# Four small moves in the backward pass of a two-layer linear-attention and gated-GLU kernel: filler units, small products, and a bank for the last quarter

## The chip, the cores and the metric

The kernel runs on one core of one Trainium2 chip. The metric is the device time of one execution in microseconds. Three runs of the kernel before gave 1201.79, 1202.06 and 1202.13 us, so the median is 1202.06 us.

## The reference

The reference computes a forward pass over a sequence of 2048 rows of width 512 and all gradients of it. The forward pass is four residual layers, A, B, A, B, that share one set of weights for A and one for B. Cut to what matters:

```python
def A(x, wqkv, wo):                     # 32 heads of 16, no softmax
    q, k, v = split_heads(x @ wqkv)
    pq, pk = phi(q), phi(k)             # phi: t+1 if t>0 else exp(t), plus 1e-6
    kv = einsum("sd,se->de", pk, v)     # per head
    den = pq @ pk.sum(s) + 1e-6
    return merge_heads((pq @ kv) / den) @ wo

def B(x, wg, wu, wd):                   # hidden width F = 1376
    return (sigmoid(x @ wg) * (x @ wu)) @ wd

x = x + A(ln(x)); x = x + B(ln(x)); x = x + A(ln(x)); x = x + B(ln(x))
return x, vjp(grad_out) w.r.t. x, wqkv, wo, wg, wu, wd
```

All inputs and outputs are bf16. Since layers 0 and 2 share their weights, and layers 1 and 3 theirs, each weight gradient is a sum over two layers.

## The kernel before, in words

The 2048 rows are cut into 16 row tiles of 128 (`st`). The residual stream and, later, its gradient stay in SBUF in float32; what the backward pass needs of each layer is stored to HBM in the forward pass.

The backward pass goes through layers 3, 2, 1, 0. `b_bwd_p1` (layers 3 and 1) and `a_bwd_p1` (layers 2 and 0) carry the gradient of x through a layer, one row tile after another. The weight gradients need all 16 row tiles of a layer at once. They are computed by one object, `W` of class `P2`, which holds a list of jobs and cuts each into **units**: sixteen matmuls of 256 or 96 columns for `wu`, `wg` and `wqkv`, eight of 512 columns for `wd`. `W.run(n)` emits the next n units at that place of the program. So units serve as filler: one is put wherever the chain of a layer would make TensorE wait. Two units in a row (a half job) share one PSUM tile of the pool `u`, which has two. After the second of them the tile is evacuated: by ScalarE (line 1386) where the result is a partial sum to be stored in HBM, by VectorE (line 1384) where it is the final one and the partial sum of the other layer is added. The result tile `dw_stg` has two buffers and is stored when its job is done, and the operand `p_set` of a job (1 MB for 256 columns) has three buffers and is loaded two jobs ahead.

All engines but SyncE run in the order in which the program text emits instructions (`tc.manual_schedule`), so the order written out by hand is the order on the chip. All DMAs are issued by SyncE (SP), in an order that the framework chooses at build time; an SP instruction that waits holds up those behind it.

The places that the change touches:

- `a_bwd_p1`, second half. `chain_mm(i, "N")` and `chain_mm(i, "M")` make two 512x512 products (line 1598, line 1602) in four tiles each, taken in turn from the pools `g` and `t`; the tiles are copied to SBUF by ScalarE and VectorE in turn (lines 362 and 364). Then the loop over row tiles begins with transposes into a tile of pool `t` (line 1649), a copy by ScalarE that seeds a tile of pool `g` (line 1633), and matmuls that add to that seed (line 1653). In its first pass one unit follows (line 1673).
- `b_bwd_p1`, layer 1. A row tile begins with three products `dhh` of 512, 512 and 352 columns (line 1059, "slices" 0, 1, 2) into the two tiles of pool `g`, each read twice by VectorE (line 1067). In the first row tile two units follow after the third slice and two more after the first transposes.
- The end of the program. After layer 0 the remaining units run without a chain beside them, 58 of them after the last loads: 42 of `wu`/`wg` (the last eight of 96 columns) and 16 of `wqkv`. Among them stand eight small products `sg` (`a_small_grads`: lines 1719 and 1728, into pool `t`, evacuated by ScalarE to a two-buffer tile `fin_o` at lines 1721 and 1731, then stored at 1722 and 1732).
- The very last job is `split`: its third and fourth quarter (16 matmuls each) are evacuated and stored on their own, but both lie in one PSUM tile (lines 1404 to 1413).

Of the kernel before, what the change touches and what calls it, by code (L numbers as in the profile page):

```python
# [10 lines left out]
F32 = mybir.dt.float32  # L11
# [11 lines left out]
P = 128  # L23
NST = S // P
NDC = D // P
# [37 lines left out]
def ps_tile(k, which, shape, dt, name):  # L63
    return k.ps[which].tile(shape, dt, name=name, tag="ln_tp" if which == "ln" else f"{which}_ps")
# [3 lines left out]
def kernel(  # L68
# [22 lines left out]
    k = K()  # L91
# [147 lines left out]
    if True:  # L239
        def load_b_weights():  # L240
            k.wdT = wb.tile([P, NDC, F], BF16, name="wdT", tag="w_c")
            nc.sync.dma_start(out=k.wdT[:], in_=k.wT["wdT"].rearrange("(c p) f -> p c f", p=P))
            k.wuT = wb.tile([P, NFC, D], BF16, name="wuT", tag="w_a")
            k.wgT = wb.tile([P, NFC, D], BF16, name="wgT", tag="w_b")
            for t_sb, t_d in ((k.wuT, k.wT["wuT"]), (k.wgT, k.wT["wgT"])):
                nc.sync.dma_start(out=t_sb[:], in_=t_d.rearrange("(c p) j -> p c j", p=P))

        def load_a_weights(l):
            woT_GT = wb.tile([P, 2, NDC, D], BF16, name="woT_GT", tag="w_b")
            k.woT, k.GT = woT_GT[:, 0, :, :], woT_GT[:, 1, :, :]  # L250
            nc.sync.dma_start(out=k.woT, in_=k.wT["woT"].rearrange("(c p) j -> p c j", p=P))
            k.wqkvT = wb.tile([P, 3 * NDC, D], BF16, name="wqkvT", tag="w_a")
            nc.sync.dma_start(out=k.wqkvT[:], in_=k.wT["wqkvT"].rearrange("(c p) j -> p c j", p=P))
            MT_X = wb.tile([P, 2, NDC, D], BF16, name="MT_X", tag="w_c")
            k.MT, k.X_ld = MT_X[:, 0, :, :], MT_X[:, 1, :, :]
            nc.sync.dma_start(out=k.MT, in_=k.sv[l]["MT"].rearrange("(c p) j -> p c j", p=P))
            nc.sync.dma_start(out=k.X_ld, in_=k.sv[l]["X"].rearrange("(c p) j -> p c j", p=P))
        k.load_b_weights, k.load_a_weights = load_b_weights, load_a_weights

        bconst = bctx.enter_context(tc.tile_pool(name="bconst", bufs=1, reuse_waits="tile"))  # L260
        k.ident32 = bconst.tile([P, P], F32, name="ident32")
        nc.gpsimd.memset(k.ident32[:], 0.0)
        nc.gpsimd.affine_select(out=k.ident32[:], in_=k.ident32[:], compare_op=ALU.not_equal, fill=1.0,
                                base=0, pattern=[[-1, P]], channel_multiplier=1)
        k.e0 = bconst.tile([P, P], BF16, name="e0")
        nc.gpsimd.memset(k.e0[:], 0.0)
        nc.gpsimd.memset(k.e0[0:1, :], 1.0)
        R = P2Res(k,
                  big=bctx.enter_context(tc.tile_pool(name="p2pool", bufs=1, reuse_waits="tile")),
                  sets=bctx.enter_context(tc.tile_pool(name="p2sets", bufs=3, reuse_waits="tile")),  # L270
                  stage=bctx.enter_context(tc.tile_pool(name="p2stage", bufs=2, reuse_waits="tile")),
                  set_w=2 * P)
        def mk_out1_cb(o1stg):
            o1cur = {}

            def out1_cb(st):
                if st % 2 == 0:
                    o1cur["t"] = o1stg.tile([P, 2, D], BF16, name="out1_t")
                nc.gpsimd.tensor_scalar(o1cur["t"][:, st % 2, :], k.xs[st][:], 1.0, 0.0, ALU.mult, ALU.add)
                if st % 2 == 1:  # L280
                    nc.sync.dma_start(out=dram_batch(out1, st // 2, 2), in_=o1cur["t"][:])
            return out1_cb

        W = P2(k, R)

        def mid3(st):
            if 4 <= st < 8:
                W.load(3, "g", part=st - 4)
            elif st == 8:
                W.add(b_jobs(k, 3), 3, False)  # L290
            elif 9 <= st < 13:
                W.load(3, "h", part=st - 9)

        def mid1(st):
            if 6 <= st < 10:
                W.load(2, "h", part=st - 6)
            elif st == 11:
                W.add(a_jobs(k, 2), 2, False)

        b_bwd_p1(k, 3, W, mid3)  # L300
        prectx.close()
        a_bwd_p1(k, R, 2, W)
        W.run(W.left() - HOLD)
        b_bwd_p1(k, 1, W, mid1)
        W.add(b_jobs(k, 1), 1, True)
        a_bwd_p1(k, R, 0, W, mk_out_cb=mk_out1_cb)
        tail = bctx.enter_context(tc.tile_pool(name="t_big", bufs=1, reuse_waits="tile"))
        W.add(a_jobs(k, 0), 0, True, split=True)
        with tc.manual_schedule(engines=EM):
            W.run(W.left() - 58)  # L310
            W.load(0, "h", tail)
            W.run(10)
            sg = a_small_grads(k, tail, R.stage)
            next(sg)
            W.run(20)
            for _ in sg:
                W.run(2)
            W.run(W.left())


# [52 lines left out]
def dram_batch(ap2d, b, nb=NB):  # L373
    return ap2d[batch_rows(b, nb), :].rearrange("(n p) d -> p n d", p=P)
# [714 lines left out]
def b_bwd_p1(k, l, W, mid):  # L1089
    nc, tc = k.nc, k.tc  # L1090
    sv = k.sv[l]
    first = k.g_from_input == l
    if not first:
        k.load_b_weights()
    with ExitStack() as ctx:
# [93 lines left out]
        def last_transposes(T):  # L1189
            transposes(T, 2)  # L1190
            store(T)
# [10 lines left out]
        for st in range(NST):  # L1202
            load(st + 1)
            ssd, h_st = LD.pop(st)
            T = dict(st=st, h=h_st, ssd=ssd, dd=halved(st, "dd", wide))
            T["ddT"] = wide.tile([P, 2, NFC, P], BF16, name="ddT")
            for fs in range(2):
                if not (first and st == 0):
                    dd_ops(k, T["dd"], T["ssd"], fs, dhh_mm(k, gTs[st], fs))
                if st == 1 and fs == 0:  # L1210
                    last_transposes(p1)
            if p2 is not None:
                p2["ln"].sums()
            if p1 is not None:
                dh_mm(p1, 0, NFC)
                transposes(T, 0)
            ps = dhh_mm(k, gTs.pop(st), 2)
            dd_ops(k, T["dd"], T["ssd"], 2, ps)
            g_tile(st + 2)
            gT_make(st + 1)  # L1220
            if p1 is None:
                if not first:
                    W.run(2)
                transposes(T, 0)
                if not first:
                    W.run(HOLD - 4)
            else:
                dh_mm(p1, NFC, NFC + 5)
            if p2 is not None:
                p2["ln"].add()  # L1230
            transposes(T, 1)
            if p1 is not None:
                dh_mm(p1, NFC + 5, 2 * NFC)
                ln_begin(p1)
                last_transposes(T)
            p1, p2 = T, p1
# [66 lines left out]
class P2:  # L1303
# [67 lines left out]
    def units(self):  # L1371
        k, R, nc = self.k, self.R, self.k.nc
        i = 0
        while True:
            j = self.jobs[i]
# [12 lines left out]
            if nm == "wd":  # L1388
                n = (w + P - 1) // P
                for c in range(n):  # L1390
                    r = min(P, w - c * P)
                    ps = k.ps["u"].tile([P, 512], F32, name="p2_ps", tag="u_ps")
# [9 lines left out]
            else:  # L1402
                for half in range(2):
                    ps = k.ps["u"].tile([P, 512], F32, name="p2_ps", tag="u_ps")
                    for icl in range(2):
                        ic = half * 2 + icl
                        for st in range(NST):
                            nc.tensor.matmul(ps[:, icl * w:(icl + 1) * w],  # L1408
                                             lhsT=self.ops[j["l"], "h"][:, st, ic * P:(ic + 1) * P],
                                             rhs=set_t[:, st, 0:w], start=(st == 0), stop=(st == NST - 1))  # L1410
                        if j["split"] and half == 1:
                            evac(ic * w, w, ps[:, icl * w:(icl + 1) * w])
                            self.io(j, dst, ov, True, (ic, ic + 1))
                        if icl == 0:
                            yield
                    if not (j["split"] and half == 1):
                        evac(half * 2 * w, 2 * w, ps[:, 0:2 * w])
                    if j["split"] and half == 0:
                        self.io(j, dst, ov, True, (0, 2))
                    if half == 1 and not j["split"]:  # L1420
                        self.io(j, dst, ov, True)
                    yield
# [13 lines left out]
def a_bwd_p1(k, R, l, W, mk_out_cb=None):  # L1436
# [6 lines left out]
    with ExitStack() as ctx:  # L1443
# [9 lines left out]
        with tc.tile_pool(name=f"ab_stg1{l}", bufs=3, side="right", reuse_waits="tile") as stg, \  # L1453
# [75 lines left out]
            for jc in range(NDC):  # L1529
# [3 lines left out]
                ps = ps_tile(k, "g", [P, D], F32, "GT_ps")  # L1533
# [10 lines left out]
        with tc.tile_pool(name=f"ab_stg2{l}", bufs=2, side="right", reuse_waits="tile") as stg, \  # L1544
# [66 lines left out]
            W.run(1)  # L1611
            for i in range(NDC):
                chain_mm(i, "M")

            def finish(T):
                st = T["st"]
# [147 lines left out]
```

## Time and profile before

| | before |
|---|---|
| median of three runs | 1202.06 us |
| profiled execution, its own time | 1202.16 us |
| its span, first to last instruction | 1200.4 us |
| TensorE (PE) busy | 1169.6 us, 97% of the span |
| VectorE (DVE), ScalarE (ACT), GpSimd (POOL) busy | 730.6, 593.2, 290.2 us |
| granted TensorE clock | 1.000 |
| share of the chain that ended last on PE | 92% |

A row of the timeline gives start, duration, engine, line, operation, output and input tiles, shapes and count, then in brackets the idle time of the engine just before and what ended it. Rows of equal instructions are merged. The end of a matmul is modelled, so successive PE rows overlap in the print. Some matmul records are missing, which shows in the counts.

### The profile page before, as it was taken

What the parts mean: (1) busy time and instruction counts of PE and PEld (TensorE: products, weight loads), DVE (VectorE), ACT (ScalarE), POOL (GpSimd) and SP (SyncE); (2) the same over time, 40 slices, a digit from 0 to 9 for tenths busy, and PEclk for the clock granted to TensorE, in tenths of its full rate; (3) what the DMA queues carried; (4) which work ended last, traced back from release to release, by engine and by line L of the source; (5) the groups of instructions that cost most, each with busy time, mean ns of one, the idle gap of its engine ahead of it and who ended that gap; (6) DMA issues with size and microseconds to landing.
All of it is one profiled execution on the core that took longest, in us unless ns stands there. A gap on an engine that the chain in (4) does not pass through costs nothing.

```text
span 1200.4 us, 21734 instructions
## 1 busy us (share of the span) xinstructions
PE 1169.6 (97%) x8185; PEld 717.5 (60%) x8302; DVE 730.6 (61%) x1414; ACT 593.2 (49%) x1100; POOL 290.2 (24%) x498
## 2 busy tenths in 40 slices
PE   8989999998999999999999999999999999999998
PEld 4445555444555555555546568865556745547887
DVE  6788886777777556665884760056664976751111
ACT  6667776547766644444635641144444625630010
POOL 5646665425666410000110010000100110110000
PEclk9999999999999999999999999999999999999999
DMA  8834455434546777977765859558897685749874
GB/s 263 290 136 156 168 180 183 154 137 165 188 149 232 237 228 249 336 217 222 239 190 165 263 172 315 136 161 261 256 298 224 207 275 164 231 117 350 258 208 151
DMA packets 266233, 256.05 MB, mean 213 GB/s; under 512 B 43280, under 2 KB 251024, under 8 KB 261264
## 3 DMA queue, kind: packets, MB, share of 16 engines
q1 hardware_dynamic: 266128, 254.65, 66.5%
q8 instruction: 65, 1.06, 0.4%
q14 instruction: 40, 0.33, 0.1%
HBM read 135.69 MB, written 118.92 MB: 212 GB/s over the span
## 4 chain that ended last, share of the span: by engine, by line
PE 92%; DVE 4%; ACT 2%; issue 1%; DMA 1%; another core or an unknown queue 0%; SPq 0%; ACTq 0%; DVEq 0%
PE p_ps L1408 17%; PE dh_ps L1174 13%; PE dh_ps L1622 7%; PE p_ps L1394 6%; PE dhh_ps L1059 6%; PE u_ps L909 6%; PE g_ps L909 6%; PE y_ps L935 6%; PE T_ps L1134 3%; PE GT_ps L1535 2%; PE y_ps L854 2%; PE dp_ps L1510 2%; PE dpk_ps L1653 2%; PE t_mm L604 2%; PE t_tp L923 2%; PE X_ps L612 1%
## 5 line engine op out<-in xcount | busy, mean ns | idle before, releaser
L1408 PE MATMUL p_ps<-p_set,p_a 128*128 128x256 bf16 (+1 forms) x2048 | 211.7, 264 | 0.6 <-DVE dw_stg L1384 0.5
L1408 PEld LDWEIGHTS <-p_a 128*128 128x128 bf16 x2048 | 185.9, 98 | 22.5 <-issue 0.7
L1067 DVE TENSOR_TENSOR dd<-dhh_ps,ssd 128x512 bf16<-128x512 f32 x144 | 82.5, 629 | 136.7 <-PE dhh_ps L1059 131.8
L1138 ACT COPY ddT<-T_ps 128x1024 bf16<-128x1024 bf16 (+1 forms) x96 | 83.0, 867 | 124.7 <-PE T_ps L1134 124.3
L1033 POOL TENSOR_SCALAR ab<-c 128x2 f32<-128x2 f32 x64 | 12.3, 192 | 436.4 <-DVE junk L1030 405.1
L915 POOL TENSOR_TENSOR ssd_t<-hh_t,oms 128x512 bf16<-128x512 bf16 (+1 forms) x96 | 101.7, 1064 | 55.5 <-ACT out_t L219 41.1
L1174 PEld LDWEIGHTS <-ddT 128*128 128x128 bf16 (+1 forms) x704 | 67.7, 98 | 69.3
L909 PEld LDWEIGHTS <-hT 128*128 128x128 bf16 x768 | 71.1, 98 | 56.6 <-DVE hT L362 1.0
L1384 DVE TENSOR_TENSOR dw_stg<-p_ps,dw_stg 128x512 bf16<-128x512 f32 (+3 forms) x44 | 28.5, 649 | 109.4 <-PE p_ps L1408 84.2
L909 PE MATMUL g_ps<-wg,hT 128*128 128x512 bf16 (+1 forms) x381 | 89.6, 357 | 0.8 <-DVE hT L362 0.6
L909 PE MATMUL u_ps<-wu,hT 128*128 128x512 bf16 (+1 forms) x384 | 90.0, 357 | 0.0
L914 DVE TENSOR_TENSOR hh_t<-u_ps,ssd_t 128x512 bf16<-128x512 f32 (+1 forms) x96 | 61.0, 636 | 45.9 <-PE u_ps L909 24.5
L1174 PE MATMUL dh_ps<-wgT,ddT 128*128 128x512 bf16 (+1 forms) x352 | 86.2, 379 | 0.0
L1174 PE MATMUL dh_ps<-wuT,ddT 128*128 128x512 bf16 (+1 forms) x351 | 81.2, 379 | 0.1
L1394 PE MATMUL p_ps<-p_a,p_set 128*128 128x512 bf16 (+1 forms) x343 | 79.9, 379 | 0.5
L1025 ACT ACTIVATE t_sb<-dh_ps,rstd_all 128x512 f32<-128x512 f32 x64 | 44.0, 687 | 71.2 <-issue 38.4
L1059 PE MATMUL dhh_ps<-wdT,gT 128*128 128x512 bf16 (+1 forms) x341 | 75.8, 355 | 2.1 <-DVE dd L1067 0.5
L935 PE MATMUL y_ps<-wd,hhT 128*128 128x512 bf16 (+1 forms) x322 | 75.1, 379 | 2.2 <-DVE x L937 0.6
L1030 DVE SCALAR_TENSOR_TENSOR junk<-t_sb,h_ld 128x512 bf16<-128x512 f32 x64 | 44.0, 688 | 48.7 <-ACT t_sb L1025 46.9
L911 ACT ACTIVATE ssd_t<-g_ps 128x512 bf16<-128x512 f32 (+1 forms) x96 | 53.2, 554 | 30.8 <-PE g_ps L909 30.6
L1386 ACT CAST dw_stg<-p_ps 128x512 bf16<-128x512 f32 (+2 forms) x43 | 24.1, 560 | 67.8 <-PE p_ps L1408 61.1
L1394 PEld LDWEIGHTS <-p_set 128*128 128x128 bf16 (+1 forms) x352 | 33.6, 100 | 34.9
(239 smaller groups left out, 2158.4 us busy)
## 6 DMA issues: line engine op xcount, KB each, us to landing
p_set<-sv_hdd SPq DMA_DIRECT2D x30, 1024.0 KB, 6.4
sv_ssd<-ssd_t SPq DMA_DIRECT2D x32, 688.0 KB, 3.4
ssd<-sv_ssd SPq DMA_DIRECT2D x24, 688.0 KB, 5.2
sv_hdd<-dd SPq DMA_DIRECT2D x48, 320.0 KB, 3.6
sv_hdd<-hh_t SPq DMA_DIRECT2D x32, 320.0 KB, 2.6
h_ld<-sv_h SPq DMA_DIRECT2D x32, 256.0 KB, 5.1
p_a<-sv_h SPq DMA_DIRECT2D x16, 512.0 KB, 6.2
p_set<-sv_dqk SPq DMA_DIRECT2D x8, 1024.0 KB, 7.9
```

Of the source, the lines that this page charges most:

```text
L909: nc.tensor.matmul(ps[:, 0:w], lhsT=hT[:, kc, :], rhs=w_sb[:, kc, c0:c0 + w], start=(kc == 0), stop=(kc == NDC - 1))
L911: nc.scalar.activation(ssd_t[:, 0, c0:c0 + w], g_ps[:, 0:w], ACT.Sigmoid)
L914: nc.vector.tensor_tensor(hh_t[:, c0:c0 + w], u_ps[:, 0:w], ssd_t[:, 0, c0:c0 + w], ALU.mult)
L915: nc.gpsimd.tensor_tensor(ssd_t[:, 1, c0:c0 + w], hh_t[:, c0:c0 + w], oms[:, 0:w], ALU.mult)
L935: nc.tensor.matmul(y_ps[:], lhsT=T["hhT"][0:r, fc, :], rhs=k.wd[0:r, fc, :], start=(fc == 0), stop=(fc == NFC - 1))
L1059: k.nc.tensor.matmul(ps[:, 0:w], lhsT=gT[:, jc, :], rhs=k.wdT[:, jc, c0:c0 + w], start=(jc == 0), stop=(jc == NDC - 1))
L1067: k.nc.vector.tensor_tensor(dd[:, a, c0:c0 + w], ps[:, 0:w], ssd[:, a, c0:c0 + w], ALU.mult)
L1138: nc.scalar.copy(ddT[:, :, f0:f0 + nfull, :], tps[:, :, 0:nfull, :])
L1174: nc.tensor.matmul(T["dh"][:], lhsT=ddT_block(T, a, fc), rhs=(k.wuT, k.wgT)[a][0:r, fc, :], start=(i == 0), stop=(i == 2 * NFC - 1))
L1394: nc.tensor.matmul(ps[0:r, :], lhsT=set_t[:, st, c * P:c * P + r], rhs=self.ops[j["l"], "g"][:, st, :], start=(st == 0), stop=(st == NST - 1))
L1408: nc.tensor.matmul(ps[:, icl * w:(icl + 1) * w], lhsT=self.ops[j["l"], "h"][:, st, ic * P:(ic + 1) * P], rhs=set_t[:, st, 0:w], start=(st ...
L1622: nc.tensor.matmul(dh_ps[:], lhsT=lhsT, rhs=rhs, start=(i == 0), stop=(i == len(ops) - 1))
```

## The change

Four edits, in the order of the program's execution:

- In `a_bwd_p1` (layers 2 and 0) one unit is emitted between the M products and the loop of the second half.
- In the first row tile of `b_bwd_p1` for layer 1, one of the two units that followed the third slice now stands in front of it.
- At the end, six instead of ten units run before the loads of the small products are emitted, and three instead of two units run after each small product.
- The last quarter of the last job gets a PSUM tile of its own, from pool `g`.

The number of units, matmuls and bytes stays as it was. The unit that is now emitted earlier in `a_bwd_p1` is one less in the long run of units behind it: `W.run(W.left() - HOLD)` after layer 2, `W.run(W.left() - 58)` after layer 0.

```diff
             W.load(0, "h", tail)
-            W.run(10)
+            W.run(6)
             sg = a_small_grads(k, tail, R.stage)
             next(sg)
             W.run(20)
             for _ in sg:
-                W.run(2)
+                W.run(3)
             W.run(W.left())
...
                     dd_ops(k, T["dd"], T["ssd"], fs, dhh_mm(k, gTs[st], fs))
                 if st == 1 and fs == 0:
                     last_transposes(p1)
+                if st == 0 and fs == 1 and not first:
+                    W.run(1)
...
             if p1 is None:
                 if not first:
-                    W.run(2)
+                    W.run(1)
                 transposes(T, 0)
...
                         ic = half * 2 + icl
+                        if j["split"] and ic == NDC - 1:
+                            ps = ps_tile(k, "g", [P, 512], F32, "p2_end")
                         for st in range(NST):
...
             for i in range(NDC):
                 chain_mm(i, "M")
+            W.run(1)
 
             def finish(T):
```

## The prediction

> **What bounds the kernel.** I read the page first, then PE's waits, then the timeline around each wait that an edit touches.
>
> ```profile
> PE 1169.6 (97%) x8185; PEld 717.5 (60%) x8302; DVE 730.6 (61%) x1414; ACT 593.2 (49%) x1100; POOL 290.2 (24%) x498
> PE 92%; DVE 4%; ACT 2%; issue 1%; DMA 1%; another core or an unknown queue 0%; SPq 0%; ACTq 0%; DVEq 0%
> ```
>
> PE is the bound, and the change removes no matmul. All it can win are PE's waits. Of the table of waits, these are the ones that the edits aim at (total, times, longest):
>
> ```profile
> PE T_ps L1649 <- DVE Mv L362: 0.9, 2, 0.5
> PE sg_ps L1728 <- ACT fin_o L1731: 0.7, 1, 0.7
> PE dhh_ps L1059 <- DVE dd L1067: 0.5, 1, 0.5
> PE p_ps L1408 <- DVE dw_stg L1384: 0.5, 1, 0.5
> PE dpk_ps L1653 <- ACT dpk_ps L1633: 0.4, 1, 0.4
> ```
>
> That is 3.0 us of idle time as listed. The timeline of PE shows more. Around the start of the second half of layer 2:
>
> ```profile
> 639.30 1.03 PE L1602 MATMUL ch_ps<-wqkvT,dkvbdT 128*128 128x512 bf16 x4
> 640.68 0.38 PE L1649 MATMUL T_ps<-ident,pk_ld 128*128 128x128 bf16 x4 [0.35 <-DVE Mv L362]
> 640.90 0.39 PE L1649 MATMUL T_ps<-ident,dq_ld 128*128 128x128 bf16 x4
> 641.65 1.02 PE L1653 MATMUL dpk_ps<-Nv,hT_ld 128*128 128x512 bf16 x3 [0.37 <-ACT dpk_ps L1633]
> ...
> 644.48 0.39 PE L1649 MATMUL T_ps<-ident,pk_ld 128*128 128x128 bf16 x4
> 644.71 0.39 PE L1649 MATMUL T_ps<-ident,dq_ld 128*128 128x128 bf16 x4
> ```
>
> Unhindered, four transposes take 0.22 us from start to start (644.48 to 644.71), though each row ends after 0.39: the modelled end holds a tail of some 0.17 us in which the next matmul would already run. A wait therefore costs start to start minus the unhindered spacing, about 0.16 us more than its bracket says. The Trainium skill, "TensorE: Matmul & The Clock Gate", section "Step-by-step: what each phase is for", says the same of the array: in a stream the drain of one matmul lies under the fill of the next, and an isolated one can't hide it. By brackets alone the four covers below would be worth 2.28 us, by start to start 3.07; the rows bear out the second, and I take it.
>
> **The four covers.**
>
> *Second half of layer 2 (line 1602 on).* Four matmuls of 512 columns take 0.86 us in a stream (the `dpk` products start at 644.93, and `dh` after them at 645.79). So T_ps lost 640.68 - 639.30 - 0.86 = 0.52 and dpk 641.65 - 640.90 - 0.22 = 0.53, together 1.05 us. The new unit takes 1.745 us (periodic set loads on SP, 1131.08 and 1138.06, are four units apart). The copies waited for end at about 641.2 (Mv) and 641.6 (the seed), and PE would now ask for them at 641.9 and 642.4: both are covered, and all 1.05 goes. The unit is one less of the 38 behind the layer, a stream without waits, so it costs nothing there. The half job closes one unit earlier, in the first row tile, so ScalarE gets a 0.58 us evacuation before the copy of dkT, in front of which it sits idle 1.66 us: covered. On SP one set load and one store of a partial sum move in front of the loads of the third pair of row tiles. These were issued at 644.90 and now follow the dqk store, at about 647.5 to 650; loads of this kind land after 2.5 to 5.5 us, by 655.5 at the latest, and are wanted at 644.48 + 3 x 4.35 (the spacing of row tiles) + 0.7 = 658.2. No loss.
>
> *Second half of layer 0.* M products at 995.00, transposes at 996.54: 0.68 lost, all of it covered by a unit of 1.7 us. Here the closing evacuation is VectorE's, 0.69 us, between two `dk` products where it idles 2.37 us. No loss.
>
> *First row tile of layer 1.*
>
> ```profile
> 778.94 1.67 PE L1059 MATMUL dhh_ps<-wdT,gT 128*128 128x512 bf16 x7
> 781.13 0.76 PE L1059 MATMUL dhh_ps<-wdT,gT 128*128 128x352 bf16 x4 [0.52 <-DVE dd L1067]
> 781.73 0.39 PE L1051 MATMUL gT_ps<-ident,gstage 128*128 128x128 bf16 x4
> ```
>
> The third slice waits until VectorE has read slice 0 twice. Later, seven recorded dhh rows starting at 794.65 are followed by the next product at 796.16, 1.51 us; here that is 780.45, so 0.68 is lost. A unit of 96 columns takes 0.68 (32 matmuls between 1163.72 and 1165.08), PE asks for the tile at 781.13, when it is free: 0.68 gone, or at worst 0.6. Of what the second unit used to cover, slice 0 is ready at 781.1 and slice 1 at 782.3; the transposes now come at 782.8 and 784, so nothing opens.
>
> *The last quarter.* PE stops at 1195.04 for an evacuation in its own bank and resumes at 1195.55. The last row of the 208 started 0.26 before 1195.04, and the next was due 0.11 later, at 1194.89: 0.66 lost. A tile of pool `g`, last used a hundred microseconds earlier, needs no wait. Evacuation, store and landing behind it (1197.50 to 1199.50) all move with it.
>
> Sum: 1.05 + 0.68 + 0.68 + 0.66 = 3.07 us.
>
> **The small products: one wait for another.**
>
> ```profile
> 1159.69 0.59 PE L1719 MATMUL sg_ps<-G_ld,kvbd_ld 128*128 128x512 bf16 x2
> 1160.12 1.52 PE L1408 MATMUL p_ps<-p_set,p_a 128*128 128x96 bf16 x32
> ...
> 1165.53 1.52 PE L1408 MATMUL p_ps<-p_set,p_a 128*128 128x96 bf16 x32
> 1167.78 0.61 PE L1728 MATMUL sg_ps<-dkvbd_ld,XT_ld 128*128 128x128 bf16 x8 [0.73 <-ACT fin_o L1731]
> 1168.23 3.66 PE L1408 MATMUL p_ps<-p_set,p_a 128*128 128x256 bf16 x32
> ```
> ```profile
> 1159.89 0.34 SPq L1268 DMA_DIRECT2D p_set<-sv_dqk  x1
> 1160.61 0.38 SPq L1367 DMA_DIRECT2D out_dram<-dw_stg  x1
> ```
> ```profile
> 1166.79 0.66 DVE L1384 TENSOR_TENSOR dw_stg<-p_ps,dw_stg 128x192 bf16<-128x192 f32 x2 [2.95 <-DMA out_dram<-dw_stg]
> ```
>
> The seventh product waits: due at 1165.53 + 1.36, started at 1167.78, 0.89 lost. It needs the PSUM tile of the fifth, whose copy on ScalarE needs the `fin_o` buffer of the third, whose store is queued behind the 1 MB set load of 1159.89, which took 5.8 us. The store of the last 256-column result sits in the same queue and lands 6.1 us after its issue. Until then VectorE can't evacuate the first half of the last 96-column job (both `dw_stg` buffers are taken), which shows as 2.95 us of VectorE's idle time. PE needs that half's `u` tile for the first `wqkv` unit. Before, this cost PE nothing: evacuated at 1167.1, wanted at 1168.23.
>
> Now count from 1159.69, the end of the last 256-column unit; load and store leave at the same distance from it as before, with an empty queue ahead. Up to the first wqkv unit stand eight units of 0.68 and three small products (0.43, 0.445, 0.445): 6.76 us. The tile comes free at 1166.79 + 0.33 + 0.06 = 1167.18, so at 7.49 (0.06 as between the evacuation of 1195.07, 0.42 long, and 1195.55). PE waits 0.73. The set load itself has landed at 6.0. With three units between them the products no longer meet their own store, so 0.89 goes and 0.73 comes: 0.16 gained. Bounds: all 0.89 is gained if the store lands 0.75 us sooner; if it takes 8.1 us, the slowest of its kind between 1100 and 1199, the wait grows by 2.0 and 1.84 is lost. I take the value of the row itself, since what stands ahead in the queue is unchanged.
>
> Total 3.07 + 0.16 = 3.23. From the profiled 1202.16 us (span 1200.4) that leaves 1198.93; the median lies 0.10 lower, so 1198.8 us.
>
> **Rivals.**
>
> 1. *No wait takes the products' place.* The store lands early, and the gain is 3.07 + 0.89 = 3.96: 1198.1 us. For it: small stores on an empty queue land in 1.5 to 2.3 us (1190.55 to 1192.84). Against: around the wait all transfers land in the order of issue. The Trainium skill, "DMA: Bandwidth & Descriptors", section "Queues, rings and completion order", says that completion isn't first-in-first-out per issuing engine; by that the store could pass the load, but the trace doesn't show it here.
> 2. *Only the listed idle time goes,* PE losing its tail elsewhere: 2.28 and nothing from the products, 1199.8 us, no change. The unhindered spacing speaks against it.
> 3. *The store lands late,* at up to 8.1 us: 3.23 - 2.0 = 1.2, so 1200.8 us, no change.
> 4. *Slower: the store as the new bound.* Each microsecond that it lands later costs one. At 6.1 + 3.2 = 9.3 us after its issue the gain is used up, at 11.7 it is a loss of 2.4, 1204.5 us. For it: a small product's store and the next partial sum's load are now ordered differently around it. Against: they are issued after it, and no store in the stage took over 8.1.
> 5. *The edit does less than it says:* VectorE or ScalarE late by the extra evacuation, so a cover leaves half of the gain: 1.6 of 3.2, 1200.4 us, no change.
>
> **How the numbers follow.** About 0.2%, 2.4 us, is what a measurement of this kernel can tell from no change. Forecast 0.56, rival 1 0.12, rival 2 0.08, rival 3 0.09, rival 4 0.06, rival 5 0.09. Faster: forecast, rival 1 and the better part of rivals 3 and 5, 0.73. Same: 0.21. Slower 0.06. The range leaves out rival 4 and reaches to rivals 1 and 3 with 0.2 us for the spread of runs: 1197.8 to 1200.9.
>
> **What would show it.** In the profile after, the waits of T_ps, dpk_ps and dhh_ps, that of sg_ps, and the 0.5 at the last quarter are gone; a new one of p_ps on VectorE's dw_stg, 0.5 to 0.6 in brackets, stands before the first wqkv unit, with VectorE idle until the DMA of out_dram before it. Span about 1197.2. I am wrong if a wait on a DMA opens on PE, if that wait is over 2 us, or if the chain's stages keep their length.

## The result and the profile after

| | before | after |
|---|---|---|
| median of nine runs each, in one comparison | 1202.38 us | 1199.32 us |
| lowest to highest | 1201.79 to 1203.73 us | 1198.48 to 1201.24 us |
| profiled execution, its own time and span | 1202.16, 1200.4 us | 1199.19, 1197.5 us |

The ratio is 0.9975, with a 95% interval of 0.9965 to 0.9985: about 3.0 us faster. The forecast was 1198.8 us, within 1197.8 to 1200.9.

The head of the page of the kernel after: the engines' busy time, and the shares of the chain that ended last.

```profile
span 1197.5 us, 21853 instructions
...
PE 1175.6 (98%) x8302; PEld 717.0 (60%) x8302; DVE 730.5 (61%) x1414; ACT 593.2 (50%) x1100; POOL 290.2 (24%) x498
...
PE 93%; DVE 4%; ACT 2%; DMA 1%; issue 0%; POOL 0%; DVEq 0%; ACTq 0%
```

PE's busy time looks 6 us higher than before, yet the work is the same: the trace of before holds 8185 of the 8302 matmuls, this one all of them. So busy time says nothing here, and all readings below go by starts. The added lines shift the line numbers: 1602 is now 1606, 1649 is 1654, 1653 is 1658, 1408 is 1412, and VectorE's evacuation, 1384, is now 1386, a number that was ScalarE's before. In the table of PE's waits (total, times, longest), the five entries shown ahead of the change are gone, and one stands in their place:

```profile
PE p_ps L1412 <- DVE dw_stg L1386: 0.4, 1, 0.4
```

Now the four places in PE's timeline. First layer 2, at the start of the second half (columns as before):

```profile
639.73 1.03 PE L1606 MATMUL ch_ps<-wqkvT,dkvbdT 128*128 128x512 bf16 x4
640.59 1.91 PE L1412 MATMUL p_ps<-p_set,p_a 128*128 128x256 bf16 x16
642.34 0.39 PE L1654 MATMUL T_ps<-ident,pk_ld 128*128 128x128 bf16 x4
642.56 0.39 PE L1654 MATMUL T_ps<-ident,dq_ld 128*128 128x128 bf16 x4
642.78 1.03 PE L1658 MATMUL dpk_ps<-Nv,hT_ld 128*128 128x512 bf16 x4
643.64 1.91 PE L1412 MATMUL p_ps<-p_set,p_a 128*128 128x256 bf16 x16
645.39 0.39 PE L355 MATMUL t_ps<-ident,dkstage 128*128 128x128 bf16 x4
```

No bracket is left, and every spacing is the unhindered one: 0.86 behind the M products, 1.75 for the unit, 0.22 for each four transposes. The stage took 4.96 us from the M products to the transposes of line 355 before, and takes 5.66 now, with 1.745 us more work in it: 1.04 us of waiting is gone.

The same place in layer 0, before and then after:

```profile
995.00 1.03 PE L1602 MATMUL ch_ps<-wqkvT,dkvbdT 128*128 128x512 bf16 x4
996.54 0.38 PE L1649 MATMUL T_ps<-ident,pk_ld 128*128 128x128 bf16 x4 [0.52 <-DVE Mv L362]
996.76 0.39 PE L1649 MATMUL T_ps<-ident,dq_ld 128*128 128x128 bf16 x4
997.03 1.02 PE L1653 MATMUL dpk_ps<-Nv,hT_ld 128*128 128x512 bf16 x4
...
999.62 0.39 PE L355 MATMUL t_ps<-ident,dkstage 128*128 128x128 bf16 x4
```
```profile
993.71 1.03 PE L1606 MATMUL ch_ps<-wqkvT,dkvbdT 128*128 128x512 bf16 x4
994.57 1.89 PE L1396 MATMUL p_ps<-p_a,p_set 128*128 128x512 bf16 x8
996.30 0.39 PE L1654 MATMUL T_ps<-ident,pk_ld 128*128 128x128 bf16 x4
...
999.34 0.39 PE L355 MATMUL t_ps<-ident,dkstage 128*128 128x128 bf16 x4
```

The stage grew from 4.62 to 5.63 us with a unit of 1.73 us more in it: 0.72 us of waiting is gone.

The first row tile of layer 1:

```profile
778.11 1.89 PE L1059 MATMUL dhh_ps<-wdT,gT 128*128 128x512 bf16 x8
779.84 0.84 PE L1412 MATMUL p_ps<-p_set,p_a 128*128 128x96 bf16 x16
780.52 0.76 PE L1059 MATMUL dhh_ps<-wdT,gT 128*128 128x352 bf16 x4
```

The eight products take 1.73 and the unit 0.68, and the third slice starts at once. The tail, down to the last quarter. The last 256-column unit of `wu`/`wg` ends one 96-column unit, some 0.68 us, ahead of the first row shown, at 1158.11 (1154.62, where a row of 48 matmuls starts, and 3.49 for the 32 wide ones among them):

```profile
1158.80 0.59 PE L1724 MATMUL sg_ps<-G_ld,kvbd_ld 128*128 128x512 bf16 x2
1159.23 2.20 PE L1412 MATMUL p_ps<-p_set,p_a 128*128 128x96 bf16 x48
1161.27 0.61 PE L1733 MATMUL sg_ps<-dkvbd_ld,XT_ld 128*128 128x128 bf16 x8
1161.71 2.20 PE L1412 MATMUL p_ps<-p_set,p_a 128*128 128x96 bf16 x48
1163.75 0.61 PE L1733 MATMUL sg_ps<-dkvbd_ld,XT_ld 128*128 128x128 bf16 x8
1164.20 0.84 PE L1412 MATMUL p_ps<-p_set,p_a 128*128 128x96 bf16 x16
1165.48 3.65 PE L1412 MATMUL p_ps<-p_set,p_a 128*128 128x256 bf16 x32 [0.44 <-DVE dw_stg L1386]
...
1175.10 17.63 PE L1412 MATMUL p_ps<-p_set,p_a 128*128 128x256 bf16 x160
1192.57 1.91 PE L1412 MATMUL p_end<-p_set,p_a 128*128 128x256 bf16 x16
```

The last quarter follows its neighbour without a gap: 160 matmuls of 0.109 us end at about 1192.55. Before, it had waited 0.52 us by the bracket:

```profile
1172.17 22.87 PE L1408 MATMUL p_ps<-p_set,p_a 128*128 128x256 bf16 x208
1195.55 1.91 PE L1408 MATMUL p_ps<-p_set,p_a 128*128 128x256 bf16 x16 [0.52 <-DVE dw_stg L1384]
```

The one wait left starts at 1164.20 + 0.68 = 1164.88 and ends at 1165.48: 0.60 us from start to start, 0.44 in the bracket. What it waits for stands in VectorE's and SP's timelines (an SPq row is the issue of a DMA; its landing comes later):

```profile
1165.07 0.62 DVE L1386 TENSOR_TENSOR dw_stg<-p_ps,dw_stg 128x192 bf16<-128x192 f32 x2 [3.24 <-PE p_ps L1412]
```
```profile
1158.31 0.34 SPq L1270 DMA_DIRECT2D p_set<-sv_dqk  x1
1159.04 0.38 SPq L1369 DMA_DIRECT2D out_dram<-dw_stg  x1
```

VectorE stands still for 3.24 us and then evacuates two halves at once. The bracket names PE, but PE ended the first half at about 1163.2, long before 1165.07. What ends just ahead is the store of 1159.04: it lands at 1164.95, 5.9 us after its issue, behind the 1 MB set load of 1158.31, which landed at 1163.98. That the load ahead of it is what makes the store late is read from this order; no run issues the store without the load.

To compare whole executions I cut the span at the start of layer 2's first M product. Behind that cut, stages repeat to some 0.01 us from run to run unless an edit or a late DMA touches them; in front of it the forward pass varies by up to 1.6 us in the profiled runs here. Before, the span behind the cut was 561.15 us; after, it is 557.74. The change itself is thus worth 3.41 us, and in its profiled run 0.43 us of that was lost in a later start of the backward pass; no edit touches what lies before the cut (the last section comes back to it).

### The profile page after: what moved, and what is told of

Its sections match the earlier page's. It is cut to its first block, busy times and chain, and to the rows that moved or that the text cites. A ratio compares the mean times of both kernels' runs of the same rounds, so it can differ in the third digit from the quotient of the medians.

```text
span 1197.5 us, 21853 instructions
## 1 busy us (share of the span) xinstructions
PE 1175.6 (98%) x8302; PEld 717.0 (60%) x8302; DVE 730.5 (61%) x1414; ACT 593.2 (50%) x1100; POOL 290.2 (24%) x498
## 4 chain that ended last, share of the span: by engine, by line
PE 93%; DVE 4%; ACT 2%; DMA 1%; issue 0%; POOL 0%; DVEq 0%; ACTq 0%
PE p_ps L1412 17%; PE dh_ps L1174 13%; PE dh_ps L1627 7%; PE p_ps L1396 6%; PE dhh_ps L1059 6%; PE u_ps L909 6%; PE g_ps L909 6%; PE y_ps L935 6%; PE T_ps L1134 3%; PE y_ps L854 2%; PE GT_ps L1539 2%; PE dpk_ps L1658 2%; PE dp_ps L1514 2%; PE t_mm L604 2%; PE t_tp L923 2%; PE X_ps L612 2%
## 5 line engine op out<-in xcount | busy, mean ns | idle before, releaser
L1059 PE MATMUL dhh_ps<-wdT,gT 128*128 128x512 bf16 x372 | 82.5, 357 | 0.0
L935 PE MATMUL y_ps<-wd,hhT 128*128 128x512 bf16 (+1 forms) x352 | 81.3, 379 | 0.6 <-DVE x L937 0.6
```

Of the source, the lines that this page charges most:

```text
L935: nc.tensor.matmul(y_ps[:], lhsT=T["hhT"][0:r, fc, :], rhs=k.wd[0:r, fc, :], start=(fc == 0), stop=(fc == NFC - 1))
L1059: k.nc.tensor.matmul(ps[:, 0:w], lhsT=gT[:, jc, :], rhs=k.wdT[:, jc, c0:c0 + w], start=(jc == 0), stop=(jc == NDC - 1))
```

## The experiments

"Rest" is the span behind the cut (before 561.15, after 557.74). The first four kernels were timed in five rounds against the kernel before, which had 1202.76 us; the other four had one run each, beside one run of the kernel before of 1201.95 us, and are read by their rows alone.

**The products alone.** The kernel before with the third edit only:

```diff
-            W.run(10)
+            W.run(6)
...
-                W.run(2)
+                W.run(3)
```

> Only the spacing of the small products is changed (six units ahead of their loads, three after each). Theory (one wait for another): the wait of the seventh product is gone, a wait of p_ps on VectorE's dw_stg of 0.4 to 0.5 us (bracket) stands before the first wqkv unit, VectorE idle there until the DMA of out_dram; about 0.3 us gained, 0.03%, within noise of before. Rival (the products' wait is simply removed): 0.9 us gained and no wait on PE in that stretch. The other three waits (T_ps and dpk_ps, dhh_ps, last quarter) stay as in the kernel before.

Measured: 1203.10 us, ratio 1.0006 (0.9997 to 1.0015), rest 561.10. The wait of sg_ps is gone, and this stands in its place in PE's timeline, with VectorE's row at the same point:

```profile
1167.27 0.84 PE L1408 MATMUL p_ps<-p_set,p_a 128*128 128x96 bf16 x16
1168.79 3.65 PE L1408 MATMUL p_ps<-p_set,p_a 128*128 128x256 bf16 x32 [0.68 <-DVE dw_stg L1384]
```
```profile
1168.38 0.62 DVE L1384 TENSOR_TENSOR dw_stg<-p_ps,dw_stg 128x192 bf16<-128x192 f32 x2 [3.49 <-DMA out_dram<-dw_stg]
```

Here the trace names the store, and the other waits stand as in the kernel before. The loss is 1168.79 - 1167.27 - 0.68 = 0.84 us in place of 0.89: one wait for another, and 0.05 gained. In the kernel after the same wait cost 0.60. The order of the instructions at this place is the same, but VectorE's row comes 7.20 us behind the end of the last 256-column unit here (1161.18), against 6.96 in after: the store landed 6.2 us after its issue here and 5.9 there. The latency varies from run to run, and the expected 0.3 us, made from one run, was not reached; a gain of 0.05 us can't be told from none.

**The covers alone.** The kernel after with the old spacing (10 and 2):

```diff
-            W.run(6)
+            W.run(10)
...
-                W.run(3)
+                W.run(2)
```

> The changed kernel with the old spacing of the small products: the two units and the bank of the last quarter alone. Theory (a wait costs start to start): 1.05 + 0.68 + 0.68 + 0.66 = 3.07 us less than before, 0.25%; the wait of 0.7 us of the seventh product is back, p_ps does not wait. Rival (only the listed idle time goes): 2.28 us less. Stage by stage, from the M products to the transposes of the second row tile plus the unit: 1.05 in layer 2 and 0.68 in layer 0 by the theory, 0.72 and 0.52 by the rival.

Measured: 1199.16 us, ratio 0.9972 (0.9962 to 0.9982), rest 558.19, 2.96 us less than before. The wait of the seventh product is back, somewhat longer than before:

```profile
1164.17 1.52 PE L1412 MATMUL p_ps<-p_set,p_a 128*128 128x96 bf16 x32
1166.57 0.61 PE L1733 MATMUL sg_ps<-dkvbd_ld,XT_ld 128*128 128x128 bf16 x8 [0.88 <-ACT fin_o L1736]
```

It costs 1166.57 - 1164.17 - 1.36 = 1.04 us, 0.15 more than before. Stage by stage the covers give 1.04 in layer 2 and 0.72 in layer 0, as the theory had it within 0.04. The covers together are therefore worth 2.96 + 0.15 = 3.11 us, not the 2.28 of the brackets. By time this kernel can't be told from the kernel after.

**Three more result tiles for the last jobs.** The kernel after, with three buffers of their own for the results of the jobs that start behind the last loads:

```diff
+            R.late = tail
...
-            ov = p2_stage_tile(R, "b")
+            ov = (R.late.tile([P, NDC * R.set_w], BF16, name="dw_stg", tag="dw_late", bufs=3) if R.late
+                  else p2_stage_tile(R, "b"))
```

> The changed kernel with three result tiles dw_stg instead of two for the jobs that start after the last loads (SBUF that is free there), so that VectorE need not wait for the store of the last 256-column result. Theory: the 0.44 us wait of p_ps before the first wqkv unit is gone and 0.6 us more is gained over the changed kernel, 3.6 to 4.0 us below before. Rival: the first wqkv unit then waits for its 1 MB set load, which lands 5.9 us after the end of the last 256-column unit against 6.8 us at which the unit is due; a wait on a DMA appears and the gain is under 0.3 us.

Measured: 1198.60 us, ratio 0.9967 (0.9955 to 0.9980), rest 557.58, only 0.16 less than after. The wait on VectorE is gone, so the two result buffers were what it hung on. But some 40 us earlier another has opened (p_ps is at line 1415 in this kernel; the second row is cut off at 1140):

```profile
1086.46 35.10 PE L1415 MATMUL p_ps<-p_set,p_a 128*128 128x256 bf16 x320
1121.81 18.41 PE L1415 MATMUL p_ps<-p_set,p_a 128*128 128x256 bf16 x167 [0.26 <-DMA p_set<-sv_hdd]
```
```profile
1111.45 0.51 SPq L1722 DMA_DIRECT2D kvbd_ld<-sv_kvbd  x1
1112.00 0.92 SPq L1722 DMA_DIRECT2D dkvbd_ld<-sv_dkvbd  x1
1113.01 1.43 SPq L1272 DMA_DIRECT2D p_set<-sv_hdd  x1
```

It costs 0.26 + 0.16 = 0.42 us, and 0.60 - 0.42 = 0.18 is what remained. So neither expectation held: the wait forecast to go went, but 0.6 us was not gained, and the rival's small gain came by another load than the one it named, since the first `wqkv` unit did not wait. The set load stands behind the loads of the small products on SP and landed 8.8 us after its issue, at 1121.77. In the kernel after, the same load is issued at the same place behind them, at 1113.33, landed at 1120.71 and was wanted at about 1121.9: the margin was 1.2 us. Why the same load took 1.4 us longer in this one profiled run is open: the order on SP is the same, and the last load ahead of it was late too (6.5 us in place of 5.7).

**Four buffers for the small products' results, old spacing.** The covers alone, and in both places of `a_small_grads`:

```diff
-        o = stg.tile([P, D], BF16, name="fin_o")
+        o = pool.tile([P, D], BF16, name="fin_o", bufs=4)
```

> The changed kernel with the old spacing of the small products (ten units, then two after each), but four fin_o tiles instead of two, in SBUF that is free at the end. Theory: the seventh product no longer waits, since its tile of pool t is copied at once; five products and eight units then stand between the last 256-column unit and the first wqkv unit, 7.6 us, just past the 7.4 to 7.5 at which the u tile comes free: no wait on PE in that stretch, 3.07 + 0.89 = 3.96 us below before. Rival (the store of the last 256-column result bounds whatever is done): a p_ps wait of 0.1 to 0.4 us remains.

Measured: 1198.49 us, ratio 0.9968 (0.9957 to 0.9980), rest 557.15, 4.00 us less than before. The last small product ahead of the `wqkv` units, and those units, start without a wait:

```profile
1162.86 1.52 PE L1412 MATMUL p_ps<-p_set,p_a 128*128 128x96 bf16 x32
1164.22 0.61 PE L1733 MATMUL sg_ps<-dkvbd_ld,XT_ld 128*128 128x128 bf16 x8
1164.67 3.66 PE L1412 MATMUL p_ps<-p_set,p_a 128*128 128x256 bf16 x32
```

So the seventh product's wait did hang on the `fin_o` buffers, and five small products between the last 256-column unit and the first `wqkv` unit were enough to cover the store in this run. The margin was thin: PE asked for the tile 7.64 us after the end of the last 256-column unit, and VectorE's row came at 7.06, which by the prediction's working (0.33 + 0.06 more) frees the tile at 7.45. With the 7.35 that VectorE's row took in the covers alone, a wait of about 0.1 us would be left, by estimate. No wait is left on PE behind the cut in this run. It is the best version by the trace, 0.59 us ahead of the kernel after; the two intervals overlap, so the times don't separate them.

**The chain's unit alone, the slice's unit alone, the bank alone.** Each is the kernel before with one edit: `W.run(1)` behind the M products; the unit in front of the third slice; the tile of pool `g` for the last quarter.

> The kernel before with the unit between chain and second half alone, in layers 2 and 0. Read on the trace from the first M product of layer 2 to the end of the span (561.15 us in the kernel before). Theory (start to start): 1.05 + 0.68 = 1.7 us less, 559.4, plus or minus 0.2 for the products' wait. Rival (brackets): 1.24 less, 559.9. Rival (half covered by the extra evacuations): 0.9 less.

> The kernel before with one unit moved in front of the third slice alone. From the first gradient transposes of layer 1 to the first dh product (10.50 us in the kernel before): theory 0.68 less, 9.82; rival (brackets) 0.52 less, 9.98; rival (the unit is missed where it stood) 10.5 and a wait of T_ps.

> The kernel before with the last quarter in its own PSUM tile alone. From the last wait-free stretch of units to the start of the last quarter: theory 0.66 less than before and no wait, time from there to the end of the span unchanged at 4.9 us; rival (brackets) 0.52 less; rival (the store of the third quarter, now nearer to the last one, delays it) the 4.9 us grows by 0.3 or more.

| kernel | its time | rest | gain behind the cut | by start to start | by brackets |
|---|---|---|---|---|---|
| chain's unit alone (layers 2 and 0) | 1200.65 | 559.39 | 1.76 | 1.73 | 1.24 |
| slice's unit alone | 1201.78 | 560.49 | 0.66 | 0.68 | 0.52 |
| bank alone | 1201.95 | 560.36 | 0.79 | 0.66 | 0.52 |

The chain's unit gives its gain in the two layers (1.04 and 0.72, as in after), and the stage of layer 1's first row tile keeps its 10.50 us. In the slice's kernel that stage falls to 9.83 without a wait of T_ps, and the third slice follows directly:

```profile
779.21 1.67 PE L1059 MATMUL dhh_ps<-wdT,gT 128*128 128x512 bf16 x7
780.72 0.84 PE L1410 MATMUL p_ps<-p_set,p_a 128*128 128x96 bf16 x16
781.40 0.76 PE L1059 MATMUL dhh_ps<-wdT,gT 128*128 128x352 bf16 x4
```

Of the bank's 0.79, 0.11 is not its own: the seventh product's bracket was 0.62 in this run in place of 0.73. That leaves 0.68. The rows of the place itself agree:

```profile
1172.63 22.87 PE L1410 MATMUL p_ps<-p_set,p_a 128*128 128x256 bf16 x208
1195.34 1.91 PE L1410 MATMUL p_end<-p_set,p_a 128*128 128x256 bf16 x16
```

From the start of the 208 matmuls to the last quarter it takes 22.71 us in place of 23.38, 0.67 less, and from there to the end of the span 4.9 us as before, so the third quarter's store did not delay the last one.

**Fewer products between the store and its reader.** The kernel after with `W.run(7)` and `W.run(4)`, so that two in place of three small products lie in the stretch:

> The changed kernel with seven units ahead of the products' loads and four after each product, so that two products instead of three stand between the last 256-column unit and the first wqkv unit. Theory (the store of the last 256-column result bounds this stretch): the stretch keeps its 7.4 to 7.6 us, the bracket before the first wqkv unit grows from 0.44 to 0.9 to 1.1 us, and since the displaced product now costs its 0.44 elsewhere, the time from the first M product of layer 2 to the end grows by 0.44 over the changed kernel's 557.74. Rival (the wait depends on the spacing of products, as before the change): no wait, 0.6 us less than the changed kernel.

Measured: 1200.59 us, rest 558.23, 0.49 more than after.

```profile
1162.87 2.20 PE L1412 MATMUL p_ps<-p_set,p_a 128*128 128x96 bf16 x48
1165.99 1.91 PE L1412 MATMUL p_ps<-p_set,p_a 128*128 128x256 bf16 x16 [0.92 <-DVE dw_stg L1386]
```

The loss is 1165.99 - 1162.87 - 2.04 = 1.08 us. From the end of the last 256-column unit to the first `wqkv` unit it takes 7.39 us, against 7.37 in after and 7.61 with the products alone: the stretch has the length that the store gives it, and a product taken out of it (0.44 us) comes back as wait.

## Why the prediction was right, and where it was not

*The four covers: right, each to 0.05 us.* The rows of after give 1.04 for layer 2 (forecast 1.05); 0.72 for layer 0 (0.68; the prediction left out that the `dpk` products, too, started 997.03 - 996.76 - 0.22 = 0.05 us late there); 0.67 for the slice (0.68, the stage from the transposes of gT to the dh products falling from 10.50 to 9.83); 0.68 for the last quarter (0.66). Together 3.11 against 3.07.

*Start to start, not brackets: right.* Rival 2 would have had 2.28 for the covers. The covers alone gave 3.11, and in the single edits each wait removed gave 0.14 to 0.17 more than its bracket (1.76 against 1.24 for three waits, 0.66 and 0.68 against 0.52 for one each). That is the tail of the modelled end that the prediction read from the unhindered rows.

*The moved transfers and evacuations cost nothing: right.* In layers 2 and 0 no new wait appears on PE, so rival 5 falls: no cover was left at half its worth. The unit is paid back in full: from the transposes of line 355 in layer 2 to those of gT in layer 1 it takes 131.14 us in place of 132.88. One reading was off without a cost: ScalarE's extra evacuation does not fit into its idle time ahead of the copy of dkT but delays that copy, which starts 0.68 us behind its transposes in place of 0.42.

*One wait for another: right in mechanism and place.* The wait stood where it was forecast, on the forecast buffer, with the forecast idle time of VectorE ahead of it. Its size was 0.60 against 0.73 (0.44 in the bracket, where 0.5 to 0.6 was forecast), since the store landed 5.9 in place of 6.1 us after its issue, and the stretch took 7.37 us in place of 7.49. With the products alone the same wait cost 0.84. The old wait varies too: 0.89 before, and 1.04, 0.90, 0.92 and 0.78 with the covers, the chain's unit, the slice's unit and the bank alone. By the means of these profiled runs, a wait of 0.91 us makes room for one of 0.72, a gain of some 0.2 us, near the forecast 0.16; the 0.30 of the profiled pair is partly luck, and one pair can't settle a number of this size. Rival 1 (no wait) appeared in none of the three kernels that spread the products and keep two result buffers (after, the products alone, fewer products). Rivals 3 and 4 had the mechanism right, as the store's landing does set the length of the stretch, but the store landed 5.9 to 6.3 us after its issue in seven of the profiled runs, never the 8.1 or more that they needed.

*The sum.* 3.11 + 0.30 = 3.41 us behind the cut, against 3.23. The medians differ by 3.06 us and the two spans by 3.41 - 0.43 = 2.98; the 0.43 is the later start of the backward pass in the profiled run of after. The median came out 0.5 us above the forecast. Some 0.3 of this is the base: the forecast was set against the three runs of before shown first, 1202.06, while in the comparison before had 1202.38. The other 0.2 is within the scatter of the runs.

*What it missed.* The edit also moves the eight loads of the small products on SP. Before, a set load left every 6.99 us (1103.13, 1110.12, 1117.10), the second ahead of three of the eight. In after they run 1101.12, 1113.33, 1116.36: the second stands behind all eight and leaves 5.2 us late against that period. With the products alone it stands behind all eight as well. The prediction followed SP's queue around the store, and not here. In the profiled run of after it was covered by 1.2 us; in that with three result tiles it wasn't, and cost 0.42. The prediction named a wait on a DMA as what would show it wrong, but had not looked at the place where one nearly opened.

## What to carry to other kernels

Price a wait on TensorE from the start of the row before it to its own start, less the unhindered spacing that the same rows show elsewhere; the idle time printed beside it misses the tail of the last matmul, and over five short waits that was a quarter of the gain. When products are spread to break one buffer's cycle, count what they covered where they stood before: here they hid a store, and the store's landing, not the number of products, then set the time. Where each transfer has its own small result tile, give it enough buffers before moving work about: by the rows of one profiled run each, four buffers in place of two did more for the products than the new spacing.

## What the runs showed that was not expected

The forward pass is what scatters, and the granted clock has a part in it. Rows of windows (stretch, length, busy time of PE, PEld, DVE, ACT and POOL with counts, then the granted clock, DMA share and GB/s), of after and then of the kernel with the products alone:

```profile
60.00:63.00 3.00, 2.81 (x7) 1.04 (x8) 2.04 (x5) 1.43 (x3) 0.00 (x0) 0.50 0.31 108
```
```profile
266.50:269.50 3.00, 3.00 (x8) 1.08 (x9) 2.04 (x4) 1.17 (x2) 0.00 (x0) 0.50 0.22 78
```

In both the clock is half. In the profiled run of before the clock is 1.00 in both stretches, and in the kernel with the products alone it is 1.00 in the first. These are the ends of the k/q stages of layers 0 and 2, where PE waits again and again for small tiles. From the start of the M products to that of the next `t_mm` products the second stretch takes 3.28 us (266.43 to 269.71) at half the clock and 2.19 (266.46 to 268.65) at the full one: 1.09 us for one spell of 3.4 us (around the first stretch, the windows 57:60, 60:63 and 63:66 show 0.97, 0.50 and 0.96, together 3.42 us at half). The longest wait of PE just ahead of it is 0.56 us.

No kernel here changes the forward pass, yet of the ten profiled runs three have one such spell in layer 0, three have one in layer 2, and four, that of before among them, have none. With it the cut lies at 639.57 to 640.65 us, without it at 639.07 to 639.54. The runs' times agree: of the 20 runs of before timed beside the first four kernels, the 7 whose mean clock is below 1.000 have a median of 1203.11 us, the other 13 one of 1202.41. Of the 11 runs of the products alone, 8 have a mean clock below 1.000, which may be why its median lies above that of before although its rest does not. One spell is a third of what was to be measured.

The Trainium skill, "TensorE: Matmul & The Clock Gate", section "What's actually happening", says that the throttled state is the default, that it is half the rate, and that activity is watched over a free-running window of 3413 ns; the length and the 0.50 agree with it. What decides in which execution the spell comes was not tried.
